# The tail of a zero fill, dealt out in DMAs of few rows

## The chip, the cores and the metric

The kernel runs on one core of a Trainium2 chip. The metric is device time of one execution in microseconds (us). The core has compute engines (TensorE or PE, VectorE or DVE, ScalarE or ACT, GpSimd or POOL), SyncE (SP), which here does nothing but issue DMAs and wait, and 16 DMA engines, which move the bytes of all DMAs whoever issues them.

## The reference, cut to what matters

The reference is one decode step of a transformer block (attention over a sliding window of a key/value cache, then a gated bilinear feed-forward part) together with its backward pass: it returns the output and the gradients of eight inputs.

```python
W = min(4096, max(256, Sk // 4))          # Sk = 32768, so W = 4096
k = jnp.repeat(k_cache[:, :, Sk - W:, :], rep, axis=1)
v = jnp.repeat(v_cache[:, :, Sk - W:, :], rep, axis=1)
...
h = x + _A_ref(_layernorm(x, axis=-1), A_k_cache, A_v_cache, A_wq, A_wo)
h2 = h + _B_ref(_layernorm(h, axis=-1), B_w_gate, B_w_up, B_w_down)
```

The caches have 8 groups of 32,768 positions of 256 bf16 values. Attention sees only the last 4,096 positions of each. The gradients of the two caches (`out_2` for keys, `out_3` for values) have the caches' full shape, so for the first 28,672 positions of every group they are zeros that must be written: 8 groups x 2 caches x 14.68 MB = 234.9 MB of zeros.

## The kernel before, in words

**The fills.** `zeros` is a tile of 128 partitions x 8,192 bf16 in SBUF, cleared once (L57, L58). The loop at L59 to L62 then issues 16 DMAs on SyncE's queue (`FILL`), for each group first `out_2`, then `out_3`. One DMA writes 128 rows; a row is 7 blocks (`NZ`) of 8,192 values, 16,384 B each, all read from the same partition of `zeros`. The DMAs carry no data that anything waits for. Queue q1 in the profile is this one. The framework gives a DMA one of eight completion semaphores in turn, and a DMA on a semaphore waits until the one that had it before, eight DMAs earlier, has completed.

**Everything else that moves** goes through GpSimd's queue (`IO`, q0 in the profile): the loads of weights and cache windows (L79, 2 MB each), the small gradient outputs (L477, L501, L521) and the window gradients (L607).

**The compute.** A forward pass over the groups makes scores, softmax and moments (L322, L329), then come the feed-forward part and its backward (L413 to L445), then the loop over the groups at L560 makes the window gradients: TensorE forms them in PSUM (L602), `evac` (L208 to L213) moves them to SBUF alternately with ScalarE and VectorE, and L607 stores them, 128 rows of 16,384 B in a DMA, two DMAs for a group. After each group's stores the `side` jobs of that group issue the weight gradients. The last group has no side jobs, so its second store is the last DMA on GpSimd's queue.

**The order.** It is fixed by the program: each engine runs its own list in order, and the two DMA queues are drained side by side by the same 16 DMA engines. At the end SyncE waits for every outstanding DMA and all engines meet in a closing barrier (L635).

Of the kernel before, what the change touches and what calls it, by code (L numbers as in the profile page):

```python
# [16 lines left out]
G = 8  # L17
Dh = 256
W = 4096
T = 32  # L20
F = 1792
FC = 14
Sk = 32768
# [6 lines left out]
HF = F // 2  # L30
ZW = 8192
NZ = (Sk - W) * Dh // (128 * ZW)


K_SLOT = [5, 6, 7, 5, 6, 7, 5, 7]
# [5 lines left out]
def kernel(  # L41
# [4 lines left out]
    FILL = nc.sync  # L46
    IO = nc.gpsimd
# [8 lines left out]
    FILL.dma_start(out=go_bf[:], in_=grad_out.rearrange("a b d -> (a b) d"))  # L56
    zeros = const.tile([128, ZW], bf16)  # L57
    V_.memset(zeros[:], 0.0)  # L58
    for g in range(G):  # L59
        for o in (out_2, out_3):  # L60
            reg = o[0, g, 0:Sk - W, :].rearrange("s d -> (s d)").rearrange("(p n f) -> p n f", p=128, f=ZW)
            FILL.dma_start(out=reg, in_=zeros[:].unsqueeze(1).to_broadcast([128, NZ, ZW]))  # L62


    S = const.tile([128, NS, SLOT], bf16)
# [6 lines left out]
    def slot_kv(k):  # L72
        return S[:, k, :].rearrange("p (t d) -> p t d", d=Dh)
# [4 lines left out]
    def load_window(dst, cache, g):  # L78
        IO.dma_start(out=dst, in_=cache[0, g, Sk - W:, :].rearrange("(p t) d -> p t d", t=T))  # L79
# [128 lines left out]
    def evac(out, in_):  # L208
        if evac_ctr[0] % 2 == 0:
            S_.copy(out=out, in_=in_)  # L210
        else:
            V_.tensor_copy(out=out, in_=in_)  # L212
        evac_ctr[0] += 1  # L213
# [135 lines left out]
    for g in range(G):  # L349
# [18 lines left out]
        if g == 0:  # L368

            t = ps.tile([128, D], f32, tag="tmp", bufs=1)  # L370
# [183 lines left out]
    def vt_buf():  # L554
        k = vt_ctr[0] % 2
        vt_ctr[0] += 1
        return VTb[:, k, :].rearrange("p (i h c) -> p i h c", i=4, h=2)

    kt_buf = vt_buf
    for g in range(G):  # L560
        if g in V_AGAIN:
            Vw[g] = slot_kv(V_AGAIN[g])
        dp = bps.tile([128, T, 2], f32, tag="dp")
        for q in range(8):
            tr = ps.tile([128, 4, 2, 128], bf16, tag="tr", bufs=2)
            for i in range(4):
                for dh in range(2):
                    P_.transpose(tr[:, i, dh, :], Vw[g][:, 4 * q + i, dh * 128:(dh + 1) * 128], ident_bf[:])  # L568
            xt = vt_buf()
            evac(xt, tr[:])  # L570
            for i in range(4):
                for dh in range(2):
                    P_.matmul(dp[:, 4 * q + i, :], lhsT=xt[:, i, dh, :], rhs=doT[:, 4 * g + dh:4 * g + dh + 3:2],  # L573
                              start=(dh == 0), stop=(dh == 1))
        for again, sl in V_AGAIN.items():
            if sl == g:
                load_window(slot_kv(sl), A_v_cache, again)
        pds = small.tile([128, T, 4], bf16, tag="pds")
        V_.tensor_copy(out=pds[:, :, 0:2], in_=pT_all[:, g])
        df = small.tile([128, T, 2], f32, tag="df")  # L580
        V_.tensor_tensor(out=df[:], in0=dp[:], in1=delta[:, 2 * g:2 * g + 2].unsqueeze(1).to_broadcast([128, T, 2]), op=ALU.subtract)
        V_.tensor_tensor(out=pds[:, :, 2:4], in0=df[:], in1=pT_all[:, g], op=ALU.mult)
        r_ps = ps.tile([128, 128], bf16, tag="tmp", bufs=1)
        P_.transpose(r_ps[:], pds[:].rearrange("p t r -> p (t r)"), ident_bf[:])
        rows = rowb[:, g % 2]
        V_.tensor_tensor(out=rows, in0=r_ps[:].unsqueeze(1).to_broadcast([128, 8, 128]), in1=mrow[:].unsqueeze(2).to_broadcast([128, 8, 128]), op=ALU.mult)
        R_ps = ps.tile([128, 2 * Dh], f32, tag="tmp", bufs=1)
        for k, (E, rr) in enumerate(((Ed, do_rows), (Eq, q_rows))):
            ex = small.tile([H, 32, 4], bf16, tag="ex")
            V_.tensor_copy(out=ex[:], in_=E[:, g, :].unsqueeze(1).to_broadcast([H, 32, 4]))  # L590
            P_.matmul(R_ps[:, k * Dh:(k + 1) * Dh], lhsT=ex[:].rearrange("h a r -> h (a r)"), rhs=rr[:], start=True, stop=True)
        R = small.tile([128, 2 * Dh], bf16, tag="R")
        S_.copy(out=R[:], in_=R_ps[:])
        sv = slot_kv(STG[(2 * g) % 4])
        sk = slot_kv(STG[(2 * g + 1) % 4])
        stg = [sv, sk]
        for c in range(T // 2):
            d_ps = bps.tile([128, 2, 2, Dh], f32, tag="d2", bufs=2)
            for i in range(2):
                t = 2 * c + i  # L600
                k, a = t // 8, t % 8
                P_.matmul(d_ps[:, i, :, :].rearrange("p w d -> p (w d)"), lhsT=rows[32 * k:32 * k + 32, a, :], rhs=R[32 * k:32 * k + 32, :],  # L602
                          start=True, stop=True)
            for w in range(2):
                evac(stg[w][:, 2 * c:2 * c + 2, :], d_ps[:, :, w, :])
        for w, o in ((0, out_3), (1, out_2)):
            IO.dma_start(out=o[0, g, Sk - W:, :].rearrange("(p t) d -> p t d", t=T), in_=stg[w])  # L607
        for job in side[g]:
            job()


# [28 lines left out]
```

## Time and profile before

| | us |
|---|---|
| median of 3 runs (lowest, highest) | 816.41 (816.31, 818.14) |
| the profiled execution's own time | 816.48 |
| its span, first to last instruction | 814.7 |
| last window store issued (L607) | 761.9 |
| last packet of the last fill ends | 813.1 |

| | |
|---|---|
| busy share of the span: PE, DVE, ACT, POOL | 62%, 46%, 20%, 5% |
| DMA packets and bytes over the span | 24,573 packets, 338.66 MB, mean 416 GB/s |
| median time of a fill from issue to landing | 149.7 us |

How to read it: busy shares are of instructions that compute; DMAs have rows of their own. The page divides the span into 40 slices and gives the mean busy share of the 16 DMA engines in each, in tenths. A window of the trace gives the same share for any stretch, beside the bytes moved in it. The trace also has a record for each DMA packet with its queue, start, duration and size, without the number of the DMA engine that moved it; a packet of 4 B is the write of a completion semaphore, and each of the 16 engines in a DMA makes one.

### The profile page before, as it was taken

The page shows a single profiled execution, that of the slowest core. Times are in us where ns is not written, and L with a number is a line of the kernel's source. Part 1 is how long each engine was busy: PE and PEld are TensorE (multiplying, and loading weights), DVE is VectorE, ACT ScalarE, POOL GpSimd, SP SyncE. Part 2 cuts the span into 40 slices and gives each one's busy share as a digit, 9 for nine tenths or more (in the row PEclk, how much of TensorE's full clock was granted, in tenths as well). Part 3 has the DMA queues.
Part 4 walks back from the last instruction along what each step waited for, and adds up shares of the span by engine and source line. Part 5 has one row for each costly group of instructions (what it writes and reads, how often), then busy time and mean ns, then how long its engine had stood idle before and what let it go on. Part 6 is the DMA issues. An engine that isn't in the chain of part 4 may idle for free.

```text
span 814.7 us, 12155 instructions
## 1 busy us (share of the span) xinstructions
PE 504.1 (62%) x4991; PEld 301.7 (37%) x4991; DVE 374.4 (46%) x1149; ACT 165.0 (20%) x261; POOL 40.4 (5%) x75
## 2 busy tenths in 40 slices
PE   3559969999566947062995562597597848263200
PEld 3445646666434524031983421243143313010000
DVE  4128837776451644028733470754553626253200
ACT  0230211221101000001012231243343424142100
POOL 3000000000000001000001000001000010000000
PEclk9959878999785969565556555555555555555555
DMA  8999999999999999999999999999999999999993
GB/s 344 430 423 427 430 428 429 425 428 426 430 417 426 415 424 420 428 429 431 426 427 429 409 415 421 431 423 422 404 430 425 425 413 423 421 425 427 424 427 170
DMA packets 24573, 338.66 MB, mean 416 GB/s; under 512 B 1251, under 2 KB 1317, under 8 KB 4677
## 3 DMA queue, kind: packets, MB, share of 16 engines
q1 hardware_dynamic: 14596, 234.88, 68.3%
q0 software_dynamic: 9920, 103.00, 30.2%
q8 instruction: 39, 0.64, 0.3%
q14 instruction: 18, 0.14, 0.0%
HBM read 57.28 MB, written 280.59 MB: 415 GB/s over the span
## 4 chain that ended last, share of the span: by engine, by line
issue 59%; DMA 17%; PE 11%; DVE 4%; POOL 3%; ACT 1%; POOLq 0%; DVEq 0%
DMA S<-in_A_wo_dram 4%; DMA Rt<-in_A_wq_dram 4%; DMA out_dram<-Mt 3%; PE dq_ps L453 3%; DMA S<-in_A_k_cache_dram 3%; DMA S<-in_A_v_cache_dram 2%; PE MT L322 2%; POOL out_dram L477 1%; POOL S L79 1%; DVE Rt L423 1%; POOL out_dram L607 1%; PE dh_ps L159 1%; PE d_ps L602 1%; PE tr L568 1%; PE t L413 1%
## 5 line engine op out<-in xcount | busy, mean ns | idle before, releaser
L602 PE MATMUL d_ps<-R,Mt 32*128 32x512 bf16 x256 | 124.4, 612 | 94.4 <-DVE S L212 93.6
L322 PE MATMUL MT<-Rt,S 128*128 128x512 bf16 x512 | 156.8, 391 | 21.1 <-DMA S<-in_A_v_cache_dram 19.9
L318 DVE TENSOR_SCALAR Rt<-S,pf 128x256 bf16<-128x256 bf16 x512 | 117.8, 283 | 32.0 <-PE acc L329 17.3
L212 DVE CAST S<-d_ps 128x512 bf16<-128x512 f32 x128 | 86.8, 689 | 57.1 <-ACT S L210 43.9
L210 ACT CAST S<-d_ps 128x512 bf16<-128x512 f32 x128 | 75.1, 587 | 171.6 <-PE d_ps L602 171.6
L266 PE MATMUL tr<-ident_bf,S 128*128 128x128 bf16 x512 | 52.5, 267 | 44.5 <-DMA S<-in_A_k_cache_dram 41.2
L602 PEld LDWEIGHTS <-Mt 32*128 32x128 bf16 x256 | 23.2, 113 | 148.1 <-issue 146.7
L325 PEld LDWEIGHTS <-S 128*128 128x128 bf16 x512 | 49.9, 98 | 62.7 <-issue 6.6
L568 PE MATMUL tr<-ident_bf,S 128*128 128x128 bf16 x512 | 68.8, 304 | 3.5 <-ACT Mt L210 3.5
L329 PE MATMUL acc<-ones_bf,Rt 128*128 128x1 bf16 x1024 | 61.8, 163 | 0.0
L568 PEld LDWEIGHTS <-S 128*128 128x128 bf16 x512 | 48.5, 135 | 28.0 <-issue 27.8
L266 PEld LDWEIGHTS <-S 128*128 128x128 bf16 x512 | 41.4, 121 | 42.9 <-DMA S<-in_A_k_cache_dram 41.7
L210 ACT COPY Rt<-tr 128x1024 bf16<-128x1024 bf16 x32 | 32.4, 1012 | 84.7 <-PE tr L266 84.3
L325 PE MATMUL acc<-pT_all,S 128*128 128x2 bf16 x512 | 49.1, 165 | 0.0
L329 PEld LDWEIGHTS <-Rt 128*128 128x128 bf16 x1024 | 44.5, 96 | 0.0
L212 DVE COPY Rt<-tr 128x1024 bf16<-128x1024 bf16 x32 | 22.1, 690 | 48.5 <-PE tr L266 47.0
L210 ACT COPY Mt<-tr 128x1024 bf16<-128x1024 bf16 x32 | 32.4, 1014 | 56.3 <-PE tr L568 29.2
L322 PEld LDWEIGHTS <-S 128*128 128x128 bf16 x512 | 32.0, 97 | 21.7 <-DMA S<-in_A_v_cache_dram 20.4
L331 ACT COPY Mt<-MT 128x512 f32<-128x512 f32 x8 | 4.7, 586 | 164.8 <-PE MT L322 145.4
L573 PEld LDWEIGHTS <-Mt 128*128 128x128 bf16 x512 | 19.9, 108 | 36.7 <-DVE Mt L212 13.7
L573 PE MATMUL dp<-doT,Mt 128*128 128x2 bf16 x512 | 22.6, 168 | 12.3 <-DVE Mt L212 10.5
L212 DVE COPY Mt<-tr 128x1024 bf16<-128x1024 bf16 x32 | 22.0, 686 | 16.4 <-PE tr L568 11.3
(182 smaller groups left out, 435.1 us busy)
## 6 DMA issues: line engine op xcount, KB each, us to landing
out_dram<-zeros SPq DMA_DIRECT2D x16, 14336.0 KB, 149.7
out_dram<-S POOLq DMA_DIRECT2D x16, 2048.0 KB, 29.5
S<-in_A_v_cache_dram POOLq DMA_DIRECT2D x11, 2048.0 KB, 35.6
S<-in_A_k_cache_dram POOLq DMA_DIRECT2D x8, 2048.0 KB, 28.0
out_dram<-Mt POOLq DMA_DIRECT2D x6, 896.0 KB, 22.3
S<-in_A_wq_dram POOLq DMA_DIRECT2D x1, 3584.0 KB, 14.7
S<-in_A_wo_dram POOLq DMA_DIRECT2D x2, 1792.0 KB, 35.4
out_dram<-Mt POOLq DMA_DIRECT2D x3, 1024.0 KB, 35.7
```

The source lines that it names most:

```text
L79: IO.dma_start(out=dst, in_=cache[0, g, Sk - W:, :].rearrange("(p t) d -> p t d", t=T))
L210: S_.copy(out=out, in_=in_)
L212: V_.tensor_copy(out=out, in_=in_)
L266: P_.transpose(tr[:, i, dh, :], Xw[:, 4 * q + i, dh * 128:(dh + 1) * 128], ident_bf[:])
L318: V_.tensor_scalar(out=pk[:, i, h, :], in0=K[:, t, :], scalar1=pf[:, t, h:h + 1], scalar2=None, op0=ALU.mult)
L322: P_.matmul(MT[:, hf, :], lhsT=Vv[:, t, hf * 128:(hf + 1) * 128], rhs=pk[:, i, :, :].rearrange("p h d -> p (h d)"), start=(t == 0), stop=( ...
L325: P_.matmul(acc[:, 2 * hf:2 * hf + 2], lhsT=Vv[:, t, hf * 128:(hf + 1) * 128], rhs=pT_all[:, g, t, :], start=(t == 0 and hf == 0), stop=(t ...
L329: P_.matmul(acc[:, 4 + 2 * h + dk:5 + 2 * h + dk], lhsT=pk[:, i, h, dk * 128:(dk + 1) * 128], rhs=ones_bf[:, 0:1], start=False, stop=(t == ...
L453: P_.matmul(dq_ps[:, 2 * h + dk:2 * h + dk + 1], lhsT=Mt[:, h // 2, hf, c0:c0 + 128], rhs=doT_f[:, 2 * h + hf:2 * h + hf + 1], start=(hf = ...
L568: P_.transpose(tr[:, i, dh, :], Vw[g][:, 4 * q + i, dh * 128:(dh + 1) * 128], ident_bf[:])
L573: P_.matmul(dp[:, 4 * q + i, :], lhsT=xt[:, i, dh, :], rhs=doT[:, 4 * g + dh:4 * g + dh + 3:2], start=(dh == 0), stop=(dh == 1))
L602: P_.matmul(d_ps[:, i, :, :].rearrange("p w d -> p (w d)"), lhsT=rows[32 * k:32 * k + 32, a, :], rhs=R[32 * k:32 * k + 32, :], start=True, ...
```

## The change

The last of the 16 fills (`out_3` of the last group, 14.68 MB) is cut into pieces. The first two are 128-row DMAs from `zeros` on SyncE's queue: 5 blocks of 8,192 values to a row, and one of 5,824. Then come seven DMAs on SyncE's queue with 14, 12, 10, 8, 6, 4 and 3 rows (590 KB together), and two on GpSimd's queue with 4 rows and with 12 rows of 12 pieces (2.1 MB together). These nine read their zeros not from `zeros` but from the region of `out_2` that the first fill has written. The two on GpSimd's queue are issued behind the last window store, one after the other. No other instruction is changed, and none changes its place in its engine's list.

```diff
+TAIL_SYNC = [(14, 1, 7168), (12, 1, 6144), (10, 1, 5632), (8, 1, 4096), (6, 1, 3072), (4, 1, 2176), (3, 1, 1536)]
+TAIL_POOL = [(4, 1, 6144), (12, 12, 7168)]
...
+    late_fills = []
     for g in range(G):
         for o in (out_2, out_3):
-            reg = o[0, g, 0:Sk - W, :].rearrange("s d -> (s d)").rearrange("(p n f) -> p n f", p=128, f=ZW)
-            FILL.dma_start(out=reg, in_=zeros[:].unsqueeze(1).to_broadcast([128, NZ, ZW]))
+            flat = o[0, g, 0:Sk - W, :].rearrange("s d -> (s d)")
+            if g < G - 1 or o is out_2:
+                parts = [(128, NZ, ZW)]
+            else:
+                parts = [(128, 5, ZW), (128, 1, 5824)] + TAIL_SYNC + TAIL_POOL
+            a = 0
+            for p, n, f in parts:
+                dst = flat[a:a + p * n * f].rearrange("(p n f) -> p n f", p=p, f=f)
+                if p == 128:
+                    FILL.dma_start(out=dst, in_=zeros[:, 0:f].unsqueeze(1).to_broadcast([128, n, f]))
+                else:
+                    src = out_2[0, 0, 0:Sk - W, :].rearrange("s d -> (s d)")[0:p * (n + 1) * ZW]
+                    src = src.rearrange("(p n f) -> p n f", p=p, f=ZW)[:, 0:n, 0:f]
+                    if (p, n, f) in TAIL_POOL:
+                        late_fills.append((dst, src))
+                    else:
+                        FILL.dma_start(out=dst, in_=src)
+                a += p * n * f
...
         for w, o in ((0, out_3), (1, out_2)):
-            IO.dma_start(out=o[0, g, Sk - W:, :].rearrange("(p t) d -> p t d", t=T), in_=stg[w])
+            last = IO.dma_start(out=o[0, g, Sk - W:, :].rearrange("(p t) d -> p t d", t=T), in_=stg[w])
...
+    for dst, src in late_fills:
+        with tc.issue_after(last.ins):
+            last = IO.dma_start(out=dst, in_=src)
```

A triple is rows, pieces in a row, values in a piece (2 B each).

More of the change, by code (lines that the diff above doesn't have):

```diff
@@ L58 @@
     V_.memset(zeros[:], 0.0)
+    late_fills = []
     for g in range(G):
         for o in (out_2, out_3):
-            reg = o[0, g, 0:Sk - W, :].rearrange("s d -> (s d)").rearrange("(p n f) -> p n f", p=128, f=ZW)
-            FILL.dma_start(out=reg, in_=zeros[:].unsqueeze(1).to_broadcast([128, NZ, ZW]))
+            flat = o[0, g, 0:Sk - W, :].rearrange("s d -> (s d)")
[16 more added lines that the diff above has]
+                a += p * n * f
+            assert a == (Sk - W) * Dh
     S = const.tile([128, NS, SLOT], bf16)
```

## Prediction

> **What bounds the kernel now.** I read the page first: busy shares, slices, DMA queues. No compute engine is over 62% busy, while the DMA row is full from the second slice to the last but one.
>
> ```profile
> span 814.7 us, 12155 instructions
> ...
> DMA  8999999999999999999999999999999999999993
> ...
> q1 hardware_dynamic: 14596, 234.88, 68.3%
> q0 software_dynamic: 9920, 103.00, 30.2%
> q8 instruction: 39, 0.64, 0.3%
> ```
>
> The reader is to see a kernel bound by its 16 DMA engines: q1 holds SyncE's zero fills, q0 the loads and stores that GpSimd issues, q8 instruction fetches. Compute done sooner would gain nothing. The chain of waits does not help here: its largest part is "issue" (59%), since it stops at POOL's closing drain. So I went to SyncE's waits, and then to the windows of the last microseconds.
>
> ```profile
> SPq L635 <- DMA out_dram<-zeros: 52.7, 2, 44.8
> ```
>
> From 768.6 to 813.5 us SyncE waits for the last fill alone. The windows (the last two columns are DMA share and GB/s) show how that fill ends:
>
> ```profile
> 780.00:796.00 16.00, 0.00 (x0) 0.00 (x0) 0.00 (x0) 0.00 (x0) 0.00 (x0) 0.50 1.01 428
> 796.00:800.00 4.00, 0.00 (x0) 0.00 (x0) 0.00 (x0) 0.00 (x0) 0.00 (x0) 0.50 0.86 369
> 800.00:804.00 4.00, 0.00 (x0) 0.00 (x0) 0.00 (x0) 0.00 (x0) 0.00 (x0) 0.50 0.46 197
> 804.00:808.00 4.00, 0.00 (x0) 0.00 (x0) 0.00 (x0) 0.00 (x0) 0.00 (x0) 0.50 0.17 74
> 808.00:813.10 5.10, 0.00 (x0) 0.00 (x0) 0.00 (x0) 0.00 (x0) 0.00 (x0) 0.50 0.06 26
> ```
>
> The engines stop one after another; 0.06 is one of sixteen. The unused share is 4 x 0.14 + 4 x 0.54 + 4 x 0.83 + 5.1 x 0.94 = 10.8 us: with all engines stopping together the last packet would end near 802.3, not 813.1. That is all a better balance can give (1.3%).
>
> The trace's packet records agree. The last fill's sixteen completion writes come at 796.9, 797.1, six from 799.6 to 800.7, four from 803.1 to 803.6, then 805.0, 807.6, 807.7 and 813.1. One is always far behind: it trails the last but one by 4.4 us in fill 4, 8.1 in fill 8, 12.7 in fill 12. Packets follow back to back, so they can be joined into 16 chains; up to 690 us the same chain is late in every fill, with no instruction fetch on it. The records do not give an engine's number. That is the gap in what follows.
>
> **The change, part by part.** Its own time is 816.48 us, 3.4 us after the last packet at 813.1; the median, 816.41, is the same for my purpose. So time = end of last packet + 3.4. Price of bytes: 428 GB/s over 16 engines is 26.8 GB/s each, 37.4 ns per KB.
>
> *Taken from every engine.* The last fill had 7 blocks of 16,384 B for each of 8 rows per engine; now 5, and one of 11,648 B. That is 8 x (2 x 16,384 - 11,648) = 168,960 B less: -6.3 us on all sixteen.
>
> *Seven small DMAs on SyncE's queue.* How few rows are dealt out is seen at one place: the 896 B load of one row is one packet with one completion, the 896 B store that goes out as 16 rows is 16 packets of 56 B on 16 engines. So I take one row per engine. 14 rows reach at most 14 engines, 3 rows three. An engine in all seven gets 14,336 + 12,288 + 11,264 + 8,192 + 6,144 + 4,352 + 3,072 = 59,648 B, 2.2 us; one in none gets 0.
>
> *Two DMAs on GpSimd's queue.* Four engines get 12,288 B (0.5 us), if no others; twelve get 12 x 14,336 = 172,032 B (6.4 us), what was taken off them. If the two deal to separate engines, the four are about 5.9 us lighter than the twelve. If both count from the same first engine, four get both and four get neither.
>
> *Copies from memory to memory.* The new DMAs read zeros from out_2; the trace has none such. Nearest below: a 16 KB packet into or out of SBUF, 0.61 us either way, factor 1.0; no reason I see makes a copy cheaper. Nearest above: the instruction fetches, 0.3% x 16 x 814.7 us / 0.64 MB = 61 ns per KB, factor 1.6, but they go to another kind of memory. I take 1.0, the row nearest in size and queue, and keep 1.6 for the range. The Trainium skill, "DMA: Bandwidth & Descriptors", "Latency and other measured facts", gives copies between HBM tensors 214 GB/s per direction at best; by that the factor would be about 2.0 and the sum that of rival 3 or worse. No run here shows it.
>
> *Issue and waits.* SyncE ends its last fill issue at 694.2 and then only waits; seven issues at 0.2 to 0.3 us (rows of L54, L56) are 2 us in 119 idle ones. Each carries a wait for the DMA eight places before it. The 4-row one waits for fill 15 (all engines done at 768.1); the 3-row one, last in the queue, for the 5-block piece of fill 16. On the late engine that piece ends one 8 x 11,648 B piece (3.5 us) before its own last zero, so near 803.5; x_bf took 0.9 us from issue to end, so the 3 rows land near 805. That is hidden by at least 1.5 us of the late engine; without that cover it would cost those 1.5. POOL's two issues (0.53 us each, row of L607) come at 762.4 with nothing behind them but its drain; the stores ahead of them in q0 land by 798.4. By the completion records their semaphores' earlier DMAs are out by then, and fill 1, which they read, landed near 68 us. All of it costs 0. If POOL's copies end last, its drain adds: it ended 0.95 us after the stores landed, so some 0.4 us in all.
>
> *Sum.* No other engine's instruction order changes. If the late engine is not among the twelve: 813.1 - 6.3 + (0 to 2.2) + (0 to 0.5) = 806.8 to 809.5. Next in line are the two at 807.6 and 807.7; among the twelve they end at 807.8 to 810.0. The later of the two ends is between 807.8 and 810.0, and I take 808.8: 808.8 + 3.4 = **812.2 us**, -0.5%. Its own range is 810.2 (807.7 lightened too, the late one with nothing added) to 813.8.
>
> **The rivals.**
>
> 1. *The forecast: the late engine is spared.* For: one engine alone owns the last 5 us, so whatever lightens it moves the end. Against: the trace does not say which it is.
>
> 2. *The late engine is among the twelve.* It is given back in q0 what q1 loses: 813.1 - 6.3 + 6.4 + (0 to 2.2) = 813.2 to 815.4, so 816.6 to 818.8 us: no gain, at most +0.3%. For: twelve of sixteen is the blind draw. Against: the small DMAs need not deal in turn. The Trainium skill, "DMA: Bandwidth & Descriptors", speaks for it: "Why a DMA increments its semaphore by 16 and not by 1" has GpSimd's DMAs with few rows take consecutive engines from a round-robin cursor, and SyncE's the lowest-numbered; "Latency and other measured facts" calls engines 7 and 15 usually the slower. From a cursor at 0 the four would be engines 0 to 3 and the twelve would hold both 7 and 15. That one engine is persistently slow the trace bears out; its number it does not.
>
> 3. *Slower: the memory-to-memory copies cost more than a fill's bytes.* Place: the twelve rows behind the final store, 172,032 B per engine with nothing left to overlap them. At factor 1.6, late engine among the twelve: 813.1 - 6.3 + 1.6 x (6.4 to 8.6) = 817.0 to 820.6, so 820.4 to 824.0 us. It is slower by 0.3% (2.4 us) from a factor of about 1.17 on there, with half of the small rows. With the late engine spared, the two at 807.7 would decide: 807.7 - 6.3 + 1.6 x (6.4 to 8.6) = 811.6 to 815.2, 815.0 to 818.6 us, no change; they are slower by 0.3% from about 1.9. For: such a copy reads and writes the same memory, and twelve engines would ask 2 x 12 x 26.8 = 643 GB/s of it, against 428 seen. Against: loads and stores run mixed at the full rate.
>
> 4. *It does not do what it says:* the copies wait and start late, or deal to fewer engines. A single engine with all 2.06 MB of the 12 rows would take 77 us, 60 us slower. The 16-row store on 16 engines speaks against it.
>
> **How the numbers follow.** 0.3%, about what a measurement of this kernel can tell from no change, is 2.4 us. Where the rows go is nearly a coin toss for me; I lean a little to the late engine spared, as two of three ways of dealing (both from a first engine and it is a high one; in turn and it is one of the four; in turn and it is one of the twelve) leave it light. The copy's factor is near 1 in somewhat more than half of my cases with either. Forecast 0.50 (faster). Rival 2 with factor near 1: 0.22 (same); spared with factor near 1.6: 0.03 (same). Rival 3: 0.24, rival 4: 0.01 (slower). Faster 0.50, same 0.25, slower 0.25. The range goes from 809.5, under the forecast's own 810.2 by the spread of packet times, to 820.0, all of rival 2 and the lower edge of rival 3; some 2 in 10 are left out, nearly all above.
>
> **What would show it.** In the windows after 796 us of the changed kernel, the share should fall steeper and later, with no 5 us at 0.06. In the packet records, the last fill's pieces must end near 807 on the late engine. The sizes 14,336 and 12,288 B tell the copies: durations near 0.53 and 0.46 us mean factor 1.0, near 0.85 and 0.73 mean 1.6. If the last packet is one of 14,336 B on q0 and the engine was late before, rival 2 holds. The forecast is wrong if the copies take much over 0.6 us, or if the last chain carries twelve of them.

## The result and the profile after

The changed kernel takes 818.50 us (median of 16 runs, 818.29 to 819.16), the kernel before 816.50 in the same runs. The ratio is 1.0024, 95% interval 1.0016 to 1.0032: slower by 2.0 us, where 0.5% faster was forecast. The time lies inside the stated range, in the part of it that was there for rival 2. The profiled execution took 818.35 us, its span is 816.6, and its last packet ends at 815.3, 2.2 us after that of before.

The page's first line and its DMA queues, after:

```profile
span 816.6 us, 12122 instructions
...
DMA  8999999999999999999999999999999999999993
...
q1 hardware_dynamic: 14598, 232.77, 67.5%
q0 software_dynamic: 10160, 105.11, 30.8%
```

The reader is to see that 2.11 MB moved from q1 to q0, as the change says, and that the DMA row is as full as before. The windows of the last microseconds (last two columns: DMA share, GB/s):

```profile
780.00:796.00 16.00, 0.00 (x0) 0.00 (x0) 0.00 (x0) 0.00 (x0) 0.00 (x0) 0.50 0.96 392
796.00:800.00 4.00, 0.00 (x0) 0.00 (x0) 0.00 (x0) 0.00 (x0) 0.00 (x0) 0.50 0.71 279
800.00:804.00 4.00, 0.00 (x0) 0.00 (x0) 0.00 (x0) 0.00 (x0) 0.00 (x0) 0.50 0.60 252
804.00:808.00 4.00, 0.00 (x0) 0.00 (x0) 0.00 (x0) 0.00 (x0) 0.00 (x0) 0.50 0.29 125
808.00:812.00 4.00, 0.00 (x0) 0.00 (x0) 0.00 (x0) 0.00 (x0) 0.00 (x0) 0.50 0.14 57
812.00:815.50 3.50, 0.00 (x0) 0.00 (x0) 0.00 (x0) 0.00 (x0) 0.00 (x0) 0.50 0.06 25
```

The fall begins earlier (0.96 and 0.71 where before had 1.01 and 0.86) and lasts longer. One engine alone still owns the end (0.06 is one of sixteen). Some engines stop sooner than before and others later.

The packet records tell who has what, since the new DMAs have sizes of their own. Packets that follow back to back are joined into chains, and a chain is taken as one engine. From 788 us on:

```
chains   last packet ends   12 rows (14,336 B, q0)   4 rows (12,288 B, q0)   small pieces on q1
  2      790.2, 793.1       none                     none                    none
  2      794.9, 794.9       none                     none                    the 14-row one
  1      815.3              twelve pieces            none                    14- to 6-row, not 4, not 3
  4      805.3 to 811.4     twelve pieces            one piece               14- to 4-row
```

(Seven more chains lie between; the row of four leaves out the 3-row pieces, which end at 811.4.) The four engines with the 4-row copy have all of the 12-row copy too. So both of GpSimd's DMAs count from the same first engine, as SyncE's do, and rows go to engines in order: whoever has a piece of a DMA with few rows has one of each DMA with more. First, fourth and fifth engine are meant in this order; the records have no numbers. The four that get neither are the four that get least from SyncE, and they stop at 790 to 795, the first of all. The late chain ends at 815.3 with twelve pieces and five of the seven small ones. (In q0 not every packet of 4 B is a completion write: there are 92 more than before, 1,052 against 960, where two DMAs on sixteen engines make 32. The other 60 fit one for each of the twelve engines without a 4-row piece and twelve for each of the four without a 12-row piece; that is inferred from the count.)

### The profile page after: what moved, and what is told of

Read it like the earlier page. It is cut to its first block, busy times and chain, and to the rows that moved or that the text cites. A ratio compares the mean times of both kernels' runs of the same rounds, so it can differ in the third digit from the quotient of the medians.

```text
span 816.6 us, 12122 instructions
## 1 busy us (share of the span) xinstructions
PE 503.3 (62%) x4947; PEld 303.0 (37%) x4991; DVE 375.0 (46%) x1149; ACT 164.9 (20%) x261; POOL 41.6 (5%) x77
## 4 chain that ended last, share of the span: by engine, by line
issue 58%; DMA 16%; PE 11%; DVE 4%; POOL 3%; ACT 1%; POOLq 0%; DVEq 0%
DMA S<-in_A_wo_dram 4%; DMA Rt<-in_A_wq_dram 4%; DMA out_dram<-Mt 3%; PE dq_ps L473 3%; DMA S<-in_A_k_cache_dram 3%; DMA S<-in_A_v_cache_dram 2%; PE MT L342 2%; POOL out_dram L497 1%; POOL out_dram L627 1%; POOL S L99 1%; DVE Rt L443 1%; PE dh_ps L179 1%; PE ao L403 1%; PE d_ps L622 1%; PE tr L588 1%
## 5 line engine op out<-in xcount | busy, mean ns | idle before, releaser
L342 PE MATMUL MT<-Rt,S 128*128 128x512 bf16 x468 | 146.6, 390 | 21.4 <-DMA S<-in_A_v_cache_dram 20.4
```

The source lines that it names most:

```text
L342: P_.matmul(MT[:, hf, :], lhsT=Vv[:, t, hf * 128:(hf + 1) * 128], rhs=pk[:, i, :, :].rearrange("p h d -> p (h d)"), start=(t == 0), stop=( ...
```

## The experiments

Every kernel was timed beside the kernel before on the same chip. "Late" is the engine that ends last; the before of these runs is 816.45 (first four) and 816.33 (last three). The diffs are against the changed kernel, but for two that are against the kernel before: the whole last fill copied, and half of the partitions as source. Some diffs show the new lines alone.

**GpSimd's two copies alone.** The small rows' bytes go back into the 128-row piece.

```diff
-TAIL_SYNC = [(14, 1, 7168), ... (3, 1, 1536)]
+TAIL_SYNC = []
...
-    parts = [(128, 5, ZW), (128, 1, 5824)] + TAIL_SYNC + TAIL_POOL
+    parts = [(128, 5, ZW), (128, 1, 8128)] + TAIL_SYNC + TAIL_POOL
```

> GpSimd's 4-row and 12-row copies alone; the small rows' bytes go back into the 128-row piece (8,128 values instead of 5,824). Main theory (the engine that is late anyway, the same one as before, is among the twelve and among those of most of the small DMAs; copies cost what a fill's bytes cost): it loses 8 x (2 x 16,384 - 16,256) = 132,096 B, 4.9 us, and gets 172,032 B, 6.4 us: its last packet ends 1.5 us later than before, 814.6, so 818.0 us. Rival, the price of the copies: packets of 14,336 B well over 0.54 us, and an end set by an engine that was not late before. Rival, a fixed price of nine more DMAs and of the waits ahead of the small ones: without the seven small DMAs most of the loss is gone, 816.6 to 817.0 us.

818.22 us (817.95 to 819.51), ratio 1.0023, interval 1.0013 to 1.0032. Its windows:

```profile
804.00:808.00 4.00, 0.00 (x0) 0.00 (x0) 0.00 (x0) 0.00 (x0) 0.00 (x0) 0.50 0.26 111
808.00:812.00 4.00, 0.00 (x0) 0.00 (x0) 0.00 (x0) 0.00 (x0) 0.00 (x0) 0.50 0.08 33
812.00:816.00 4.00, 0.00 (x0) 0.00 (x0) 0.00 (x0) 0.00 (x0) 0.00 (x0) 0.50 0.07 28
```

This trace is of an execution of 819.51 us, the slowest of the nine. The late engine is alone from about 809 to 816.2. It carries twelve packets of 14,336 B; the four with the 12,288 B packet carry twelve as well. The median of those packets is 0.535 us, what a fill's bytes cost. The main theory holds; a fixed price of the seven small DMAs does not, as the loss is there without them.

**The seven small DMAs alone.**

```diff
-TAIL_POOL = [(4, 1, 6144), (12, 12, 7168)]
+TAIL_POOL = []
...
-    parts = [(128, 5, ZW), (128, 1, 5824)] + TAIL_SYNC + TAIL_POOL
+    parts = [(128, 6, ZW), (128, 1, 5888)] + TAIL_SYNC + TAIL_POOL
```

> The seven small DMAs alone; GpSimd's 2.1 MB go back into the 128-row pieces (6 blocks and 5,888 values). Main theory: the late engine loses 8 x (16,384 - 11,776) = 36,864 B, 1.4 us, and gets five of the seven small pieces, 52,224 B, 2.0 us: end at 813.7, so 817.1 us. Rival, fixed price of the small DMAs and their waits: 818 us or more, with the 3-row DMA the last to land. Rival, the price of the copies: the small pieces alone cannot make more than 2.0 us even at factor 2.

816.85 us (816.63 to 817.5), ratio 1.0005, interval 0.9996 to 1.0014. By the median +0.4, expected +0.6; the interval takes in no change, so this run excludes a large fixed price and no more. In its trace the late engine again has the 14- to 6-row pieces and no 4-row one, and ends after the 3-row pieces (814.5 against 810.6).

**The same edit turned round: 4 rows for engines that are not late.**

```diff
+TAIL_SYNC = [(4, 8, 8192)]
+TAIL_POOL = []
...
+    parts = [(128, 6, ZW), (128, 1, 6144)] + TAIL_SYNC + TAIL_POOL
```

> The same kind of edit turned round: one DMA of 4 rows x 131,072 B behind the last fill on SyncE's queue, its bytes taken from the 128-row piece of all engines (6 blocks and 6,144 values). Main theory: the four engines that get it are not the late one; the late one loses 32,768 B, 1.2 us, and ends at 811.9, the four gain 3.7 us and end at 807 to 811.4: 815.2 us, 1.2 us under before. Rival, fixed price of more DMAs from memory to memory: no gain, 816.5 us or more. Rival, the price of the copies at factor 2: the four end at 812 to 816.3 and set the end, 815.5 to 819.7 us.

815.57 us (815.2 to 816.8), ratio 0.9991, interval 0.9982 to 1.0: 0.9 us less by the median, at the edge of what these runs tell from no change. In the trace of one execution (815.29) the late engine ends at 811.9, as worked out, with no piece of the four rows. One of the four ends at 811.1, the other three at 805.0 to 805.4: the second-latest engine is among the first four.

**The whole last fill copied from memory by all sixteen engines.**

```diff
-            FILL.dma_start(out=reg, in_=zeros[:].unsqueeze(1).to_broadcast([128, NZ, ZW]))
+            if g == G - 1 and o is out_3:
+                src = out_2[0, 0, 0:Sk - W, :].rearrange("s d -> (s d)").rearrange("(p n f) -> p n f", p=128, f=ZW)
+                FILL.dma_start(out=reg, in_=src)
...
```

> Before, with the whole last fill (14.7 MB, all sixteen engines alike) copied from the first fill's region of out_2 instead of from SBUF. Main theory (a copy costs what a fill costs): 64 KB packets of some 2.4 us, the same lateness, 816 to 817 us. Rival, the price of the copies: at factor 1.6 the fill's 34.3 us of engine time become 55, some 837 us; at factor 2.0 some 850 us. A little under 816 would say that the late engine is late for reading SBUF.

822.55 us (822.27 to 823.55), ratio 1.0077, interval 1.0063 to 1.009. Both sides missed. The 64 KB packets take 2.42 us at best, which is the price of a fill, but 2.78 in the mean: factor 1.15, and 1.19 for those that start between 770 and 790 us. From 790 on, as engines end, the mean is 2.44. On the late engine the fill's first seven packets take 2.7 to 3.0 us, some 3.2 us more than at best, and the last seven 2.42; fill 15 had ended on it 2.3 us later than before (770.4 against 768.1). The two make 5.5 us, and its last packet ends 5.2 us later, at 818.3. That packet is not of the fill, which ends at 812.9, about where it did, but of GpSimd's last window store: 16 KB pieces of the store took turns with 64 KB packets of the fill, and eight were left over. So the price of a copy is a real thing while all sixteen engines copy, though the packets are also four times as large as a fill's, and the two were not tried apart. In the changed kernel, where the copies come when engines fall idle, the 14,336 B packets take 0.552 us in the mean against 0.535 undisturbed: twelve of them, 0.2 us.

**3 rows for the first three engines.**

```diff
+TAIL_SYNC = [(3, 14, 8192)]
+TAIL_POOL = []
...
+    parts = [(128, 6, ZW), (128, 1, 5504)] + TAIL_SYNC + TAIL_POOL
```

> As the run with one DMA of 4 rows, with 3 rows of 229,376 B (their bytes taken from the last 128-row piece of all engines: 5,504 values instead of 8,192). Main theory (few rows go to the first engines in order, the late one is the fifth or sixth, the second-latest the fourth): the late engine loses 43,008 B, 1.6 us, and ends at 811.5; the fourth too, at 806.1; the first three gain 7.0 us, from some 803.6 to 810.6. 814.9 us, 1.6 us under before and 0.4 to 0.7 under the run with 4 rows. If the second-latest is one of the first three it ends at 814.7 and sets the end: 818.1 us.

815.04 us (814.26 to 815.74), ratio 0.9984, interval 0.9975 to 0.9993: this one beats both kernels, the one before by 1.3 us (0.16%). Its windows:

```profile
800.00:804.00 4.00, 0.00 (x0) 0.00 (x0) 0.00 (x0) 0.00 (x0) 0.00 (x0) 0.50 0.47 198
804.00:808.00 4.00, 0.00 (x0) 0.00 (x0) 0.00 (x0) 0.00 (x0) 0.00 (x0) 0.50 0.20 85
808.00:812.20 4.20, 0.00 (x0) 0.00 (x0) 0.00 (x0) 0.00 (x0) 0.00 (x0) 0.50 0.09 39
```

The fall is the one of before, cut at 812.2. The three end at 807.8 to 810.2, the late one at 812.2 with none of the three rows, and the second-latest is relieved: the fourth engine.

**5 rows, to name the late engine.**

```diff
+TAIL_SYNC = [(5, 4, 8192)]
+TAIL_POOL = []
...
+    parts = [(128, 6, ZW), (128, 1, 6912)] + TAIL_SYNC + TAIL_POOL
```

> One DMA of 5 rows of 65,536 B behind the last fill, taken from the last 128-row piece (6,912 values). It tells which engine is late: the late one had the 6-row DMA of the changed kernel and not the 4-row one, so by rows in order it is the fifth or the sixth. Fifth: it carries a 65,536 B packet and ends at 813.1 - 0.8 + 2.5 = 814.8, 818.2 us. Sixth: it carries none and ends at 812.3, 815.7 us. Rival, that few rows are dealt from some other engine on each time: the late one may carry it or not, but then the fourth-latest and later ones will not be the same as in the other runs.

A single execution: 818.23 us. The late chain carries a 65,536 B packet and ends at 814.9. In the changed kernel it had a piece of the 6-row DMA and none of the 4-row one, so by rows in order it is the fifth engine.

**Half of the partitions as source.**

```diff
...
+                a = 128 * 6 * ZW
+                FILL.dma_start(out=flat[0:a].rearrange("(p n f) -> p n f", p=128, f=ZW), in_=zeros[:].unsqueeze(1).to_broadcast([128, 6, ZW]))
+                FILL.dma_start(out=flat[a:a + 128 * ZW].rearrange("(p n f) -> p n f", p=64, f=ZW), in_=zeros[64:128, :].unsqueeze(1).to_broadcast([64, 2, ZW]))
...
```

> Before, with the last of the seven blocks of the last fill (2.1 MB) read from partitions 64 to 127 of the zeros alone, 64 rows of 32,768 B. If a row's engine goes by its place in the DMA, every engine gets 4 rows, 131,072 B as before: the same end, 816.4 us, or up to 5 us more should half the partitions feed sixteen engines at half the rate (2.1 MB are 4.9 us). If it goes by the partition, the eight engines that are early get it all: the late one loses 4.9 us and ends at 808.2, the early ones gain 4.9 and end at 802 to 806: some 811.6 us, a version that beats both kernels.

816.57 us (816.26 to 816.96), ratio 1.0003, interval 0.9995 to 1.0012. Every engine gets its share by place in the DMA, not by partition, and the late one ends at 813.0. Packets that read the upper half while most engines do take up to 2.07 us instead of 0.61. Those over 0.7 us lie between 793.6 and 809.7 us, and no loss shows at the end of the late engine, whose last packets are back at 0.61.

## Why the prediction was wrong, point by point

1. *What bounds the kernel* held. The DMA engines end one after another, one is late, and the time is its last packet plus some 3.1 us (818.35 against 815.3; before 3.4).

2. *The step that failed* is the first clause of the sum, "if the late engine is not among the twelve". It is among them. The working for the other case, rival 2, gives the measured number: 813.1 - 6.3 + 6.4 + (0 to 2.2). The trace shows five of the seven small pieces on it, 14,336 + 12,288 + 11,264 + 8,192 + 6,144 = 52,224 B, 2.0 us, so 813.1 + 0.1 + 2.0 = 815.2; measured 815.3. Rival 2 named 816.6 to 818.8 us and had a chance of 0.22. Of the prediction's signs, the last chain does carry twelve packets of 14,336 B, but the last packet is not one of them: on that engine the 12-row pieces took turns with q1, and the small pieces, last in q1, ended the chain.

3. *The reason for choosing the wrong case* was a count of ways to deal the rows, two of three leaving the late engine light. That count rested on nothing in the profile. It also left out a fourth way, both from a first engine and the late one is not a high one, and that is what happened: the late engine is the fifth. And it took the ways as equally likely, where by the prediction's own parts four engines of sixteen are spared whichever way the rows are dealt: 0.25 for an engine not known, where its chances come to 0.53 or more. Rows in order can only add to the first engines, and those are the later half: in the run of the seven small DMAs alone, where their sizes name the engines, the first eight end at 803.1 to 814.5 and the last eight at 796.7 to 801.7. (The small pieces themselves are 1.7 to 2.2 us of the first and 0 to 1.4 us of the last.) The change adds most where there was least room.

4. *The Trainium skill's rules.* In "DMA: Bandwidth & Descriptors", "Why a DMA increments its semaphore by 16 and not by 1", the rule that a DMA of few rows uses the lowest-numbered engines on SyncE's queue agrees with the pieces as far as records without engine numbers can show it: the seven DMAs reached 14, 12, 10, 8, 6, 4 and 3 engines, the fewer always among the more. Its rule that GpSimd's takes consecutive engines from a round-robin cursor would have put the 4 and the 12 rows on separate engines; the trace has all four of the 4-row pieces on engines that also carry the 12 rows. The measurement decides. (The section names an exception in which GpSimd's rows are dealt from the first engine on; that fits, and the prediction did not weigh it.) "Latency and other measured facts" calls engines 7 and 15 usually slower: here it is the fifth, if engines are numbered in the order of rows.

5. *The price of the copies* (rival 3) was mis-sized as a danger: 1.03 in the changed kernel, 1.15 in the mean with all sixteen engines copying. The Trainium skill, "DMA: Bandwidth & Descriptors", "Latency and other measured facts", has 214 GB/s per direction as the full rate of copies of 128 x 16 KiB tiles between HBM tensors. By that the factor would have been about 2.0, an estimate; no run here comes near it.

6. *Issue and waits at nothing* held, but by its cover more than by its reading. SyncE's own rows after the change (a first column is the start, the second the time in it):

```profile
640.73 75.42 SPq L73 DMA_DIRECT2D out_dram<-zeros  x2
716.20 94.17 SPq L80 DMA_DIRECT2D out_dram<-out_dram  x7
```

The last fill's two pieces are issued until 716.2, not 694.2, and the seven small ones take 94 us, not 2. Of these, 51.7 are waits:

```profile
SPq L80 <- DMA out_dram<-zeros: 51.7, 2, 40.6
```

The other 42 are the seven issues themselves. The prediction priced an issue by the two loads of one row and left aside the row of the fills. Here it is, with that of the small DMAs below it (ns: least, median, longest):

```profile
L62 SPq DMA_DIRECT2D out_dram<-zeros x16: 597/46418/62679, 5.2 to 641.0; - x16
L80 SPq DMA_DIRECT2D out_dram<-out_dram x7: 609/2181/31941, 716.2 to 809.7; - x7
```

The 3-row DMA left at 809.7, when the late engine had ended its 5-block piece (809.3), and its packets ended at 811.4 instead of near 805: the twelve rows alternate with that piece on the late engine. The cover was 3.9 us of that engine's own rest. GpSimd's closing drain ended at 811.8, also under cover.

What stays open is why the fifth engine is late. In the trace of before, by joined chains, its packets of 16 KB in q1 are longer than 611 ns by 16 ns in the median, most of them a little, where other engines have a few much longer ones; at the end, alone, it runs at 611. What stretches them was not tried.

## What to carry to other kernels

When a DMA-bound kernel ends with engines stopping one by one, find out which engine is the late one, by number, before moving bytes between them: a DMA of few rows can name the engines, as the 5-row one did here. In every run here few rows landed on the first engines, so they can even out a tail only if the engines they reach end before the late one, as the first three did. The room for it is the idle share after the first engine stops, here 10.8 us, of which 1.3 us was got with three rows.

## What the runs showed of the hardware that was not expected

Rows of a DMA go to the engines in order and from the first one: on SyncE's queue with 3 to 14 rows (the seven small DMAs have 57 rows and 57 completion writes), on GpSimd's with 4 and with 12 rows. One of sixteen engines is late in every trace here, by 4 to 15 us against the last but one in fills 3 to 15; one trace names it the fifth, two leave the fifth or the sixth. Copies from memory to memory cost as much as a fill's bytes while other engines idle (0.535 us for 14,336 B), and 1.15 times as much in the mean, in packets of 64 KB, when all sixteen copy. An engine with work from both queues takes a packet from each in turn, whatever their sizes (64 KB and 16 KB in the run with the whole fill copied). Issuing a DMA on SyncE's queue took up to 62.7 us, with fills ahead of it (L62 before). Reading half the partitions with all engines doubled some packets and more (up to 2.07 us for 16 KB) without a loss in time here.
